# Attention, mixture of experts and MLP: differences of x staged over iterations, another order at the turn to the MLP

## The chip, the cores and the metric

The kernel runs on one core of a Trainium2 chip. The metric is the device time of one execution in microseconds (us). Engines are named TensorE (PE in the rows; PEld is its weight load), VectorE (DVE), ScalarE (ACT), GpSimd (POOL) and the SyncE queue that issues DMAs (SP).

## The reference

Attention with a window of 32 keys (half of the heads plain, half with a step of 4), then a mixture of four experts with all experts applied to all tokens, then an MLP with a sigmoid gate. Sizes: 2 x 576 tokens (1152), model width 512, expert width 1024, MLP width 2048.

```python
x = attention(q, k, v)                      # 1152 x 512
p = domain_probs / (domain_probs.sum(-1, keepdims=True) + 1e-9)
out = sum(p[:, e:e+1] * (np.maximum(x @ w1[e], 0) @ w2[e]) for e in range(4))
h = out @ w_in
y = (h * (1 / (1 + np.exp(-1.702 * h)))) @ w_out
```

## The kernel before

Every matmul operand is split into a high part (rounded to the type that TensorE multiplies) and a low part (the rest), and each product is three matmuls: high by high, high by low, low by high. ScalarE makes the high parts by a copy, VectorE or GpSimd the low parts by a subtraction. The program order of every engine is written out by hand; each engine runs its own queue in order, and semaphores tie them.

**First expert.** It runs in 26 iterations (`it`) along with the last steps of attention. Iteration `it` issues the products g1 of one pair (chunk of 384 tokens, 128 columns of the width), their relu on ScalarE (L498) with the low part on VectorE (L499), and the second matmul g2 (L514 to L516) of the pair issued two iterations before (`LAG = 2`). After that come the functions that `at_it(it, ...)` has listed, and `slot(1)`, which takes all that stands in the list `queue`.

**Experts 1 to 3 and the MLP.** A block (s, c) is a piece s of 256 columns of the width (s = 4 to 15 for the experts, 16 to 23 for the MLP; S0 is 15, SM is 16) with a token chunk c (512 or 640 tokens, as halves of 256 or 320). The first matmul of a block is made with seven products instead of eight, on sums and differences of the weights (`w1_prep`: sets A and S) and on x and its differences (`t`, made by `combos` and kept as `th`, `tl`). In a block `first2` issues the products a, c_, b, d, a, c_, d (names ga, gc, gb, gd in the rows, L735) into four banks of the five-bank pool `ps`; between them ScalarE copies s1 and s5, VectorE adds u2 (L751) and s75 (L753), and the second d goes into the bank that s75 has read. `second2` is the second matmul (L809 to L811) by tiles of 128 tokens, into three banks `pa0` to `pa2`; for the experts and most of the MLP VectorE adds a tile to `acc` (L813, L818), for s = 16 ScalarE copies it (L815). In the MLP the relu is replaced by a chain of tanh (L771), cc (L774), high copy (L775) and low part (L778).

**Work beside.** `due` gives each block or second matmul some lists of functions and a number of slots; `bg` mixes the lists evenly, and one slot follows each of the seven products of a `first2` and each tile of a `second2`. The 64-bit rounds (`w64_round`) turn the MLP's weights, which come as 64-bit numbers, into 32 bits: load, two ScalarE casts (L681, L682), a shift (L687) and a merge (L691) on VectorE, an add on GpSimd (L692), and a store of the round before. There are 32 units and 33 rounds.

**x1_combos** joins high and low of the attention result (GpSimd, L581), takes four differences (VectorE, L565), two high casts (ScalarE, L567) and two low parts (VectorE, L556), for chunk c and half m of the model width. **x2_turn** does the same for the MLP's x: transposes of `acc` (TensorE, L599), evictions (ScalarE, L603), high casts (L562), low parts and differences.

Buffers that matter: pool `big` has two tiles (a set of x1 takes both; `cc` of a block takes one), `sd` three, `m` two, `hp2` three.

Of the kernel before, what the change touches and what calls it, by code (L numbers as in the profile page):

```python
# [8 lines left out]
F32 = mybir.dt.float32  # L9
# [14 lines left out]
def fused_kernel(ctx: ExitStack, tc: tile.TileContext, q, k, v, dp, w1, w2, w_in, w_out, out):  # L24
# [37 lines left out]
    ps = ctx.enter_context(tc.tile_pool(name="ps", bufs=5, space=bass.MemoryType.PSUM))  # L62
    pacc = ctx.enter_context(tc.tile_pool(name="pacc", bufs=1, space=bass.MemoryType.PSUM))
# [13 lines left out]
    xh = xp.tile([P, KT, NT], F32R, name="xh")  # L77
    xl = xp.tile([P, KT, NT], F32R, name="xl")
# [3 lines left out]
    late = {}  # L82
# [351 lines left out]


    work = {}

    def at_it(it, fn):
        work.setdefault(it, []).append(fn)

    def close_attention():
        at.close()
        for nm, n in (("th", 1), ("ns", 5), ("ss", 1), ("cv", 2), ("sd", 3), ("big", 2)):
            late[nm] = ctx.enter_context(tc.tile_pool(name=nm, bufs=n))
        late["t"] = late["th"].tile([P, 2, 4, 2, NT // 2], F32R, name="t")

    p0, p1, p2, p3 = ORDER
# [18 lines left out]
    pa = {}  # L466
# [61 lines left out]
    NF = F1 // 2  # L528
    N_ = (256, 320)
# [5 lines left out]
    queue = []  # L535
# [12 lines left out]
    def combos(c, m, xf, t, whole, lo_engines=(nc.vector, nc.vector)):  # L548

        n, t0, q0 = N_[c], T0[c], Q0[c]  # L550
        th, tl = (late["t"][:, y, :, m, q0:q0 + n] for y in range(2))
        b = [xf[:, y] for y in range(4)]
        fns = []

        def lo_(eng, out_, whole_, hi_):
            eng.tensor_tensor(out=out_, in0=whole_, in1=hi_.bitcast(F32), op=ALU.subtract)  # L556

        if whole:
            for y, l in ((0, 0), (2, 0), (3, 1)):
                kt = 2 * (y // 2) + m  # L560
                cols = slice(t0 + l * n, t0 + (l + 1) * n)
                fns.append(lambda y=y, kt=kt, cols=cols: nc.scalar.activation(xh[:, kt, cols], b[y], AF.Copy))  # L562
                fns.append(lambda y=y, kt=kt, cols=cols: lo_(lo_engines[0], xl[:, kt, cols], b[y], xh[:, kt, cols]))
        for y, (p, q_) in enumerate(((b[1], b[0]), (b[3], t[:, 0]), (b[3], b[1]), (b[2], t[:, 1]))):
            fns.append(lambda y=y, p=p, q_=q_: nc.vector.tensor_tensor(out=t[:, y], in0=p, in1=q_, op=ALU.subtract))  # L565
        for ys in (slice(0, 2), slice(2, 4)):
            fns.append(lambda ys=ys: nc.scalar.activation(th[:, ys, :], t[:, ys], AF.Copy))  # L567
            fns.append(lambda ys=ys: lo_(lo_engines[1], tl[:, ys, :], t[:, ys], th[:, ys, :]))
        return fns

    def big_pair(c, name):
        return [late["big"].tile([P, 4, 320], F32, tag="big", name=f"{x}{name}")[:, :, :N_[c]] for x in ("xf", "xt")]

    def x1_combos(c, m):

        n, t0 = N_[c], T0[c]
        xf, t = big_pair(c, f"1_{c}{m}")

        def join(j):
            parts_ = [x.bitcast(F32)[:, 2 * j + m, t0:t0 + 2 * n].rearrange("p (l n) -> p l n", l=2) for x in (xh, xl)]  # L580
            nc.gpsimd.tensor_tensor(out=xf[:, 2 * j:2 * j + 2], in0=parts_[0], in1=parts_[1], op=ALU.add)  # L581
        return [lambda: join(0), lambda: join(1)] + combos(c, m, xf, t, False)

    def x2_turn(c, m):

        n = N_[c]
        if (c, m) == (0, 0):
            xf, t = big_pair(c, f"2_{c}{m}")
        else:
            both = late["hp"].tile([P, 8, n], F32, tag="h", name=f"x2_{c}{m}")  # L590
            xf, t = both[:, :4], both[:, 4:]

        def turn_tiles(j, x0, some):
            kt = 2 * j + m
            pool, tag = (ps, "ps") if c == 0 else (pacc, f"pa{turn_[0] % 3}")
            turn_[0] += c
            pt = pool.tile([P, 512], F32, tag=tag, name=f"x2_{c}{kt}{x0}")
            for i, tt in enumerate(some):
                nc.tensor.transpose(pt[:, i * P:(i + 1) * P], acc[:, tt, kt * P:(kt + 1) * P], ident)  # L599
            for h in range(2):  # L600
                lo_, hi_ = max(x0 * P, h * n), min((x0 + len(some)) * P, (h + 1) * n)
                if lo_ < hi_:
                    nc.scalar.activation(xf[:, 2 * j + h, lo_ - h * n:hi_ - h * n], pt[:, lo_ - x0 * P:hi_ - x0 * P], AF.Copy)  # L603

        tiles = TILES[c]
        pieces = ((0, tiles),) if c == 0 else ((0, tiles[:3]), (3, tiles[3:]))
        fns = [lambda j=j, x0=x0, some=some: turn_tiles(j, x0, some) for j in range(2) for x0, some in pieces]
        return fns + combos(c, m, xf, t, True, (nc.gpsimd, nc.vector if m == 0 or c else nc.gpsimd))


    def w1_prep(s):
# [21 lines left out]
    def w2_prep(s):  # L633
        t = wst[s, 1]
        hi, lo = (wa.tile([P, 2, DM], F32R, tag="w2", bufs=4, name=f"w2{y}_{s}") for y in "hl")
        wt[s, 1] = (hi, lo)
        fns = []
        for o in range(2):
            fns.append(lambda o=o: nc.scalar.activation(hi[:, o], t[:, o], AF.Copy))  # L639
            fns.append(lambda o=o: nc.gpsimd.tensor_tensor(out=lo[:, o], in0=t[:, o], in1=hi[:, o].bitcast(F32), op=ALU.subtract))  # L640
        return fns

    def prep1(s):
        return w1_prep(s) if s < SE else []
# [200 lines left out]
    for x, step in enumerate(steps[:FIRST]):  # L845
        step()
        spin(SPIN.get(x - LEAD, 0))
        for fn in first_work.get(x - LEAD, []):
            fn()
    for x in range(4):  # L850
        at_it(17 + x, lambda x=x: queue.extend(x1_combos(x % 2, x // 2)))
    at_it(15, lambda: queue.extend(loads(NF) + [units64[0][0], units64[1][0]] + loads(NF + 1)))
    at_it(20, lambda: queue.extend(w1_prep(NF)))
    at_it(22, lambda: queue.extend(w2_prep(NF)))
    for x in range(16, len(seq)):
        at_it(x, lambda: queue.extend(w64_round()))

    for it in range(len(seq) + LAG):
        it_now[0] = it
# [9 lines left out]
        slot(1)  # L869
    assert not work, sorted(work)  # L870
    first_expert.close()
    late["hp"] = ctx.enter_context(tc.tile_pool(name="hp2", bufs=3, side=RIGHT))

    def order_of(keys):
        pe = [("1", keys[0])]
        for x in range(1, len(keys)):
            pe += [("1", keys[x]), ("2", keys[x - 1])]
        return pe + [("2", keys[-1])]
# [4 lines left out]

    pe = pe[:pe.index(("1", (S0, 0))) + 1]
    pe += [("1", (S0, 1)), ("2", (S0, 0)), ("2", (S0 - 1, 1)), ("2", (S0, 1))]
    pe += order_of([(SM, 0), (SM + 1, 0), (SM, 1), (SM + 1, 1)] + [(s, c) for s in range(SM + 2, SE) for c in range(2)])

    def due(kind, s, c):

        one = 7 + (len(TILES[1 - c]) if (s, c) != (NF, 0) else 0)  # L890
        if kind == "1":
            r64 = w64_round()
            if (s, c) == (S0, 0):
                return 7, [prep1(SM), r64, loads(SM + 1)]
            if (s, c) == (S0, 1):
                return 7, [r64]
            if (s, c) == (SM, 0):
                return 7, [x2_turn(1, 0), prep2(SM + 1), r64]
            if (s, c) == (SM + 1, 0):
                return 7, [x2_turn(1, 1), loads(SM + 2)]  # L900
            if (s, c) == (SM, 1):
                return 7, [loads(SM + 3)]
            if (s, c) == (SM + 1, 1):
                return None
            if (s, c) == (SM + 2, 0):
                return one, [prep2(s) + prep1(s + 1), loads(s + 2)]
            return one, [prep1(s + 1), r64, loads(s + 2)] if c == 0 else [prep2(s + 1), r64]
        if (s, c) == (S0, 0):
            return 4, [prep1(SM + 1)]
        if (s, c) == (S0 - 1, 1):  # L910
            return 5, [x2_turn(0, 0)]
        if (s, c) == (S0, 1):
            return 5, [x2_turn(0, 1), prep2(SM)]
        if (s, c) == (SM + 1, 0):
            return 4 + 7 + 5, [prep1(SM + 2)]
        return None

    for kind, (s, c) in pe:
# [3 lines left out]
            left[0] = todo[0]  # L922
            bg(*todo[1])
        (first2 if kind == "1" else second2)(s, c, slots)
    assert not queue


_INS = ["q", "k", "v", "moe_domain_probs", "moe_w1", "moe_w2", "moe2_w_in", "moe2_w_out"]
# [25 lines left out]
```

## Time and profile before

| | |
|---|---|
| runs | 686.49 us median of 3 (684.76 to 686.67) |
| profiled execution | 687.18 us, span of its instructions 685.2 us |
| granted TensorE clock, mean | 0.980 |
| busy share of the span | TensorE 95%, VectorE 64%, GpSimd 53%, ScalarE 43% |

A busy share is a mean over stages. TensorE is the engine with the most work, so time is lost where it waits or where its granted clock is below 1.00 (1.00 is 2.4 GHz, the lower level is 1.2 GHz).

### The profile page before, as it was taken

To read this page: it belongs to the slowest core of one execution; us is meant where nothing else is said; L and a number is where in the kernel's file an instruction comes from. 1 tells how busy PE (TensorE), PEld (TensorE's weight loads), DVE (VectorE), ACT (ScalarE), POOL (GpSimd) and SP (SyncE) were. 2 spreads that over 40 slices of the span, in tenths; PEclk is the share of its full clock that TensorE was granted. 3 is DMA by queue.
4 is the path that set the end of the run, shared out by engine and by line. 5 is a ranking of instruction groups with operands and counts; after the bars stand their busy time and mean duration, and the time that the engine had idled before them with its cause. 6 is when DMAs were issued, how large, how long until landed. Compare 5 with 4: busy or idle time off the path is not lost. (4 is left out here: it accounts for less than half of the span.)

```text
span 685.2 us, 10981 instructions
## 1 busy us (share of the span) xinstructions
PE 651.6 (95%) x4059; PEld 572.3 (84%) x4059; DVE 438.1 (64%) x878; ACT 291.5 (43%) x674; POOL 365.9 (53%) x360
## 2 busy tenths in 40 slices
PE   8899999994899999999999999998689999999997
PEld 5688888882798989989898988887678989889895
DVE  4765443467677676676767567666755576666655
ACT  5765332235453443434344343445445543444321
POOL 4432210247797676676767567785523845744300
PEclk9999999997899999999999999999799999999999
DMA  8866000531662434253233415120000110100003
GB/s 212 208 172 164 27 1 1 200 90 49 187 200 78 136 107 131 70 154 109 79 121 112 145 51 183 49 94 31 32 0 32 62 63 32 62 1 1 1 0 139
DMA packets 50070, 61.41 MB, mean 90 GB/s; under 512 B 20514, under 2 KB 32482, under 8 KB 50018
## 3 DMA queue, kind: packets, MB, share of 16 engines
q1 hardware_dynamic: 50016, 60.72, 29.4%
q8 instruction: 32, 0.52, 0.3%
q14 instruction: 22, 0.16, 0.1%
HBM read 49.96 MB, written 10.75 MB: 89 GB/s over the span
## 5 line engine op out<-in xcount | busy, mean ns | idle before, releaser
L809 PE MATMUL q<-w2h,h 128*128 128x512 f32 x360 | 142.8, 397 | 2.1 <-ACT acc L815 2.1
L810 PE MATMUL q<-w2l,h 128*128 128x512 f32 x360 | 142.7, 396 | 0.0
L811 PE MATMUL q<-w2h,h 128*128 128x512 f32 x360 | 142.6, 396 | 0.0
L813 DVE SCALAR_TENSOR_TENSOR acc<-q,pw,acc 128x512 f32<-128x512 f32 x108 | 78.7, 745 | 29.2 <-PE q L811 29.1
L754 POOL TENSOR_TENSOR cc<-s,u 128x256 f32<-128x256 f32 (+1 forms) x40 | 35.8, 894 | 94.6 <-DVE s L753 94.6
L809 PEld LDWEIGHTS q<-w2h,h 128*128 128x128 f32 x360 | 67.8, 188 | 17.2 <-ACT acc L815 2.5
L811 PEld LDWEIGHTS q<-w2h,h 128*128 128x128 f32 x360 | 67.8, 188 | 16.5
L810 PEld LDWEIGHTS q<-w2l,h 128*128 128x128 f32 x360 | 67.8, 188 | 14.7
L640 POOL TENSOR_TENSOR w2l<-st,w2h 128x512 fp32r<-128x512 f32 x40 | 53.3, 1335 | 39.1 <-ACT w2h L639 39.1
L692 POOL TENSOR_TENSOR m<-m,sd 128x512 int32<-128x512 int32 x32 | 42.1, 1314 | 53.5 <-DMA st<-in_moe_w_dram 19.8
L629 POOL TENSOR_TENSOR wsl<-ss,wsh 128x512 fp32r<-128x512 f32 x40 | 61.6, 1559 | 13.7 <-ACT wsh L628 13.7
L747 ACT ACTIVATE s<-ga 128x256 f32<-128x256 f32 (+1 forms) x40 | 16.5, 412 | 119.2 <-PE ga L735 119.2
L751 DVE TENSOR_TENSOR u<-gb,s 128x256 f32<-128x256 f32 (+1 forms) x40 | 18.3, 458 | 65.0 <-PE gb L735 61.2
L818 DVE SCALAR_TENSOR_TENSOR acc<-q,acc 128x512 f32<-128x512 f32 x63 | 42.5, 687 | 13.9 <-PE q L811 13.9
L625 POOL TENSOR_TENSOR wal<-st,wah 128x512 fp32r<-128x512 f32 (+1 forms) x40 | 47.6, 1211 | 6.6 <-ACT wah L624 6.6
L735 PE MATMUL ga<-xh,wah 128*128 128x256 f32 (+1 forms) x160 | 47.9, 299 | 0.1
L735 PE MATMUL ga<-xl,wah 128*128 128x256 f32 (+1 forms) x160 | 47.7, 298 | 0.0
L735 PE MATMUL ga<-xh,wal 128*128 128x256 f32 (+1 forms) x160 | 47.5, 297 | 0.0
L767 DVE SCALAR_TENSOR_TENSOR h<-cc,h 128x768 fp32r<-128x768 f32 (+1 forms) x24 | 37.4, 1558 | 7.2 <-ACT h L764 7.2
L764 ACT ACTIVATE h<-cc 128x768 fp32r<-128x768 f32 (+1 forms) x24 | 22.3, 928 | 43.9 <-DVE cc L788 35.9
L514 PE MATMUL pa<-wh,h 128*128 128x512 f32 x72 | 31.8, 441 | 9.5 <-ACT h L498 9.5
L621 POOL TENSOR_TENSOR ss<-st 128x256 f32<-128x256 f32 x40 | 40.4, 1009 | 0.0
(457 smaller groups left out, 1653.4 us busy)
## 6 DMA issues: line engine op xcount, KB each, us to landing
st<-in_moe_w_dram SPq DMA_DIRECT2D x32, 512.0 KB, 5.5
sd<-in_moe_w_in_dram SPq DMA_DIRECT2D x16, 512.0 KB, 4.3
sd<-in_moe_w_out_dram SPq DMA_DIRECT2D x16, 512.0 KB, 4.0
w<-m SPq DMA_DIRECT2D x32, 256.0 KB, 4.6
st<-w SPq DMA_DIRECT2D x16, 512.0 KB, 3.2
out_dram<-acc SPq DMA_DIRECT2D x9, 256.0 KB, 2.0
v10big<-in_v_dram SPq DMA_DIRECT2D x2, 144.0 KB, 3.0
v11big<-in_v_dram SPq DMA_DIRECT2D x2, 144.0 KB, 2.4
```

Source lines behind the costliest of these rows:

```text
L621: fns.append(lambda y=y, p=p, q_=q_, op=op: nc.gpsimd.tensor_tensor(out=sums[:, y], in0=p, in1=q_, op=op))
L625: fns.append(lambda dst=dst, srcs=srcs: nc.gpsimd.tensor_tensor(out=al[:, dst], in0=srcs, in1=ah[:, dst].bitcast(F32), op=ALU.subtract))
L629: fns.append(lambda dst=dst: nc.gpsimd.tensor_tensor(out=sl[:, dst], in0=sums[:, dst], in1=sh[:, dst].bitcast(F32), op=ALU.subtract))
L640: fns.append(lambda o=o: nc.gpsimd.tensor_tensor(out=lo[:, o], in0=t[:, o], in1=hi[:, o].bitcast(F32), op=ALU.subtract))
L692: nc.gpsimd.tensor_tensor(out=m.bitcast(I32), in0=m.bitcast(I32), in1=t.bitcast(I32)[:, :, 0], op=ALU.add)
L735: nc.tensor.matmul(bank_[:, :n], wz[:, y, m, :], xz, start=start and m == 0 and z == 0, stop=m == 1 and z == 2, skip_group_check=not start)
L767: nc.vector.scalar_tensor_tensor(hl[:, sub], src, 0.0, hh[:, sub].bitcast(F32), op0=ALU.max, op1=ALU.subtract)
L809: nc.tensor.matmul(pt, hi, wh[:, o, :], start=o == 0, stop=False)
L810: nc.tensor.matmul(pt, hi, wl[:, o, :], start=False, stop=False)
L811: nc.tensor.matmul(pt, lo, wh[:, o, :], start=False, stop=o == 1)
L813: nc.vector.scalar_tensor_tensor(acc[:, t, :], pt, pw[:, t, e:e + 1], acc[:, t, :], op0=ALU.mult, op1=ALU.add)
L818: nc.vector.scalar_tensor_tensor(acc[:, t, :], pt, 0.5, acc[:, t, :], op0=ALU.mult, op1=ALU.add)
```

## The change

Four things. The differences of x for the experts (`x1_combos`) are spread over three iterations per set: join in one, differences in the next, casts and low parts in the one after, starting in iterations 16, 17, 19 and 20; the sets of m = 1 get a pool of their own, `x1`, which is closed with the first expert, and the pools `cv` and `sd` open only then. The weights of block (4,0) are prepared in iterations 21 to 24 by name, not through the list. The 64-bit rounds of iterations 16 to 23 and of the blocks from (15,1) on are gone; blocks with c = 1, from (4,1) to (14,1), take two rounds, those with c = 0, from (5,0) to (15,0), one. At the turn to the MLP the second matmul of (17,0) moves ahead of the block (16,1); the transposes of chunk 1, m = 0, come after three empty slots in (16,0), their casts and differences in (17,0); those of m = 1 come in the second matmuls of (16,0) and (17,0), with banks of `ps` instead of `pa0` to `pa2`. The weights of (18,0) are prepared in the 12 slots of (17,1) and the second matmul of (16,1), before in the 16 slots that began at the second matmul of (17,0).

```diff
-        for nm, n in (("th", 1), ("ns", 5), ("ss", 1), ("cv", 2), ("sd", 3), ("big", 2)):
+        for nm, n in (("th", 1), ("ns", 5), ("ss", 1), ("big", 2)):
             late[nm] = ctx.enter_context(tc.tile_pool(name=nm, bufs=n))
+        late["x1"] = x1_pool.enter_context(tc.tile_pool(name="x1", bufs=2))
...
+        def join():
+            xf, t = big_pair(c, f"1_{c}{m}", ("big", "x1")[m])
+            for j in range(2):
+                parts_ = [x.bitcast(F32)[:, 2 * j + m, t0:t0 + 2 * n].rearrange("p (l n) -> p l n", l=2) for x in (xh, xl)]
+                nc.gpsimd.tensor_tensor(out=xf[:, 2 * j:2 * j + 2], in0=parts_[0], in1=parts_[1], op=ALU.add)
+            made.extend(combos(c, m, xf, t, False))
...
+        at_it(it, join)
+        at_it(it + 1, lambda: some(0, 4))
+        at_it(it + 2, lambda: some(4, 8))
...
-            pool, tag = (ps, "ps") if c == 0 else (pacc, f"pa{turn_[0] % 3}")
-            turn_[0] += c
+            pool, tag = (pacc, f"pa{turn_[0] % 3}") if (c, m) == (1, 0) else (ps, "ps")
+            turn_[0] += (c, m) == (1, 0)
...
-    for x in range(4):
-        at_it(17 + x, lambda x=x: queue.extend(x1_combos(x % 2, x // 2)))
-    at_it(15, lambda: queue.extend(loads(NF) + [units64[0][0], units64[1][0]] + loads(NF + 1)))
-    at_it(20, lambda: queue.extend(w1_prep(NF)))
-    at_it(22, lambda: queue.extend(w2_prep(NF)))
-    for x in range(16, len(seq)):
-        at_it(x, lambda: queue.extend(w64_round()))
+    at_it(15, lambda: queue.extend(loads(NF) + loads(NF + 1)))
+    for x, (c, m, it) in enumerate(((0, 0, 16), (0, 1, 17), (1, 0, 19), (1, 1, 20))):
+        x1_combos(c, m, it)
...
+        for x, which in enumerate(((0, 1, 2, 3, 4, 6), (5, 7, 8, 10), (9, 11))):
+            at_it(it + x, lambda which=which: some(*which))
+        at_it(it + 3, lambda: [fn() for fn in w2_prep(NF)])
+
+    first_weights(21)
...
-    pe += order_of([(SM, 0), (SM + 1, 0), (SM, 1), (SM + 1, 1)] + [(s, c) for s in range(SM + 2, SE) for c in range(2)])
+
+    pe += [("1", (SM, 0)), ("1", (SM + 1, 0)), ("2", (SM, 0)), ("2", (SM + 1, 0)), ("1", (SM, 1))]
+    pe += order_of([(SM, 1), (SM + 1, 1)] + [(s, c) for s in range(SM + 2, SE) for c in range(2)])[1:]
...
-            r64 = w64_round()
+            if (s, c) == (NF, 0):
+                return one, [prep1(s + 1), loads(s + 2) + [units64[0][0], units64[1][0]]]
+            r64 = [fn for _ in range(1 + c) for fn in w64_round()] if (s, c) <= (S0, 0) else []
...
             if (s, c) == (SM, 0):
-                return 7, [x2_turn(1, 0), prep2(SM + 1), r64]
+                turns.extend(x2_turn(1, 0))
+                return 7, [[nothing] * 3 + turns[0], prep2(SM + 1)]
             if (s, c) == (SM + 1, 0):
-                return 7, [x2_turn(1, 1), loads(SM + 2)]
+                return 7, [turns[1], loads(SM + 2)]
...
             if (s, c) == (SM + 1, 1):
-                return None
+                return one + 1, [prep1(SM + 2)]
...
+        if (s, c) == (SM, 0):
+            turns[:] = x2_turn(1, 1)
+            return 4, [turns[0]]
         if (s, c) == (SM + 1, 0):
-            return 4 + 7 + 5, [prep1(SM + 2)]
+            return 4, [turns[1]]
```

## Rows read from the trace of the kernel before

**Rows 1.** Page, busy tenths in 40 slices of 17.1 us, TensorE.
```profile
PE   8899999994899999999999999998689999999997
```
**Rows 2.** Waits of TensorE, whole span: total us, times, longest.
```profile
PE pa L514 <- ACT h L498: 9.5, 2, 6.4
PE x L599 <- ACT x L603: 6.3, 1, 6.3
PE pa L516 <- DVE h L499: 3.0, 3, 1.7
PE gd L735 <- DVE s L753: 2.2, 3, 1.1
PE q L809 <- ACT acc L815: 2.1, 1, 2.1
PE x L599 <- DVE acc L813: 1.9, 1, 1.9
```
**Rows 3.** Windows: length, busy us of each engine, granted clock, DMA.
```profile
148.55:181.67 33.12, 20.60 (x70) 15.19 (x70) 20.16 (x26) 12.83 (x24) 23.95 (x19) 0.79 0.32 95
473.00:512.20 39.20, 28.93 (x171) 27.05 (x170) 23.59 (x38) 19.83 (x46) 16.52 (x16) 0.83 0.08 27
307.53:319.30 11.77, 11.77 (x68) 10.67 (x67) 7.82 (x12) 4.47 (x8) 7.29 (x7) 1.00 0.22 77
```
**Rows 4.** Timeline of TensorE, first turn: start us, us, then idle before.
```profile
144.36 0.39 PE L514 MATMUL pa<-wh,h 128*128 128x512 f32 x1
...
148.55 0.39 PE L514 MATMUL pa<-wh,h 128*128 128x512 f32 x1
...
156.50 0.80 PE L514 MATMUL pa<-wh,h 128*128 128x512 f32 x1 [3.08 <-ACT h L498]
...
181.67 0.28 PE L735 MATMUL ga<-xh,wah 128*128 128x256 f32 x1
```
**Rows 5.** Timelines of GpSimd, VectorE and ScalarE, first turn.
```profile
150.29 2.54 POOL L581 TENSOR_TENSOR xf<-xh,xl 128x512 f32<-128x512 f32 x2
...
151.61 1.50 DVE L565 TENSOR_TENSOR xt<-xf 128x256 f32<-128x256 f32 x1 [2.24 <-POOL xf L581]
...
153.67 1.30 ACT L567 ACTIVATE t<-xt 128x512 fp32r<-128x512 f32 x2 [5.58 <-DVE xt L565]
...
155.97 0.47 ACT L498 ACTIVATE h<-g 128x384 fp32r<-128x384 f32 x1
```
**Rows 6.** Timelines of VectorE and TensorE, one odd block.
```profile
311.31 0.49 DVE L753 TENSOR_TENSOR s<-gd,s 128x320 f32<-128x320 f32 x1 [0.39 <-PE gd L735]
311.72 0.42 DVE L687 TENSOR_SCALAR m<-sd 128x512 uint32<-128x512 uint32 x1
...
313.41 0.68 DVE L691 SCALAR_TENSOR_TENSOR m<-sd,m 128x512 uint32<-128x512 uint32 x1
...
312.81 0.46 PE L735 MATMUL gd<-t,wah 128*128 128x320 f32 x2
```
**Rows 7.** Timeline of VectorE, blocks (15,0) and (15,1).
```profile
441.20 1.75 DVE L691 SCALAR_TENSOR_TENSOR m<-sd,m 128x512 uint32<-128x512 uint32 x1
...
447.55 1.47 DVE L687 TENSOR_SCALAR m<-sd 128x512 uint32<-128x512 uint32 x1
```
**Rows 8.** Chain that ended last, in order of time: start us, us.
```profile
458.76 0.87 PE x L599 x8
...
543.21 0.88 PE ga L735 x6
...
554.97 0.72 PE ga L735 x6
```
**Rows 9.** Timelines of GpSimd, ScalarE and VectorE, second turn.
```profile
476.57 1.28 POOL L556 TENSOR_TENSOR t<-x,t 128x512 fp32r<-128x512 f32 x1
...
488.26 0.84 ACT L771 ACTIVATE th<-cc 128x768 f32<-128x768 f32 x1 [2.56 <-DVE cc L788]
...
491.01 0.96 DVE L778 TENSOR_TENSOR h<-cc,h 128x768 fp32r<-128x768 f32 x1 [0.91 <-ACT h L775]
```

More of the change, by code (lines that the diff above doesn't have):

```diff
@@ L436, in fused_kernel @@
     work = {}
+    x1_pool = ExitStack()
     def at_it(it, fn):
@@ L569, in combos, with big_pair, x1_combos, some @@
         return fns
-    def big_pair(c, name):
-        return [late["big"].tile([P, 4, 320], F32, tag="big", name=f"{x}{name}")[:, :, :N_[c]] for x in ("xf", "xt")]
-    def x1_combos(c, m):
+    def big_pair(c, name, pool="big"):
+        return [late[pool].tile([P, 4, 320], F32, tag=pool, name=f"{x}{name}")[:, :, :N_[c]] for x in ("xf", "xt")]
+    def x1_combos(c, m, it):
         n, t0 = N_[c], T0[c]
[L577 to L582, printed above, removed]
+        made = []
+        def join():
[4 more added lines that the diff above has]
+            made.extend(combos(c, m, xf, t, False))
+        def some(a_, b_):
+            for fn in made[a_:b_]:
+                fn()
+        at_it(it, join)
+        at_it(it + 1, lambda: some(0, 4))
+        at_it(it + 2, lambda: some(4, 8))
     def x2_turn(c, m):
@@ L607, in x2_turn @@
         fns = [lambda j=j, x0=x0, some=some: turn_tiles(j, x0, some) for j in range(2) for x0, some in pieces]
-        return fns + combos(c, m, xf, t, True, (nc.gpsimd, nc.vector if m == 0 or c else nc.gpsimd))
+        return fns, combos(c, m, xf, t, True, (nc.gpsimd, nc.vector if m == 0 or c else nc.gpsimd))
     def w1_prep(s):
@@ L849, in fused_kernel, with first_weights, some @@
             fn()
-    for x in range(4):
-        at_it(17 + x, lambda x=x: queue.extend(x1_combos(x % 2, x // 2)))
-    at_it(15, lambda: queue.extend(loads(NF) + [units64[0][0], units64[1][0]] + loads(NF + 1)))
-    at_it(20, lambda: queue.extend(w1_prep(NF)))
-    at_it(22, lambda: queue.extend(w2_prep(NF)))
-    for x in range(16, len(seq)):
-        at_it(x, lambda: queue.extend(w64_round()))
+    at_it(15, lambda: queue.extend(loads(NF) + loads(NF + 1)))
+    for x, (c, m, it) in enumerate(((0, 0, 16), (0, 1, 17), (1, 0, 19), (1, 1, 20))):
+        x1_combos(c, m, it)
+    def first_weights(it):
+        made = []
+        def some(*which):
+            made.extend([] if made else w1_prep(NF))
+            for x in which:
+                made[x]()
+        for x, which in enumerate(((0, 1, 2, 3, 4, 6), (5, 7, 8, 10), (9, 11))):
+            at_it(it + x, lambda which=which: some(*which))
+        at_it(it + 3, lambda: [fn() for fn in w2_prep(NF)])
+    first_weights(21)
     for it in range(len(seq) + LAG):
@@ L871, in fused_kernel @@
     first_expert.close()
+    x1_pool.close()
+    for nm, n in (("cv", 2), ("sd", 3)):
+        late[nm] = ctx.enter_context(tc.tile_pool(name=nm, bufs=n))
     late["hp"] = ctx.enter_context(tc.tile_pool(name="hp2", bufs=3, side=RIGHT))
@@ L885, in fused_kernel, with nothing @@
     pe += [("1", (S0, 1)), ("2", (S0, 0)), ("2", (S0 - 1, 1)), ("2", (S0, 1))]
-    pe += order_of([(SM, 0), (SM + 1, 0), (SM, 1), (SM + 1, 1)] + [(s, c) for s in range(SM + 2, SE) for c in range(2)])
+    pe += [("1", (SM, 0)), ("1", (SM + 1, 0)), ("2", (SM, 0)), ("2", (SM + 1, 0)), ("1", (SM, 1))]
+    pe += order_of([(SM, 1), (SM + 1, 1)] + [(s, c) for s in range(SM + 2, SE) for c in range(2)])[1:]
+    turns = []
+    def nothing():
+        pass
     def due(kind, s, c):
@@ L895, in due @@
             if (s, c) == (S0, 1):
-                return 7, [r64]
+                return None
             if (s, c) == (SM, 0):
-                return 7, [x2_turn(1, 0), prep2(SM + 1), r64]
+                turns.extend(x2_turn(1, 0))
+                return 7, [[nothing] * 3 + turns[0], prep2(SM + 1)]
             if (s, c) == (SM + 1, 0):
-                return 7, [x2_turn(1, 1), loads(SM + 2)]
+                return 7, [turns[1], loads(SM + 2)]
             if (s, c) == (SM, 1):
@@ L910, in due @@
         if (s, c) == (S0 - 1, 1):
-            return 5, [x2_turn(0, 0)]
+            return 5, [sum(x2_turn(0, 0), [])]
         if (s, c) == (S0, 1):
-            return 5, [x2_turn(0, 1), prep2(SM)]
+            return 5, [sum(x2_turn(0, 1), []), prep2(SM)]
+        if (s, c) == (SM, 0):
+            turns[:] = x2_turn(1, 1)
+            return 4, [turns[0]]
         if (s, c) == (SM + 1, 0):
-            return 4 + 7 + 5, [prep1(SM + 2)]
+            return 4, [turns[1]]
         return None
@@ L924, in fused_kernel @@
         (first2 if kind == "1" else second2)(s, c, slots)
-    assert not queue
+    assert not queue and at64[0] == len(units64) + 1
 _INS = ["q", "k", "v", "moe_domain_probs", "moe_w1", "moe_w2", "moe2_w_in", "moe2_w_out"]
```

## The prediction

> **What bounds the kernel now.** I read the page first, then the waits of TensorE, then timelines around each place where it waits. The 40 slices [rows 1] show TensorE busy nearly everywhere and two holes: the tenth slice, where the first expert ends, and slices 28 to 30, the turn to the MLP. The list of what TensorE waited for [rows 2] puts causes to them: 9.5 us on ScalarE's relu of the first expert (L498) with 3.0 us on VectorE's low part (L499), then 6.3, 2.1 and 1.9 us on instructions of the second turn, and 2.2 us on VectorE's s75 (L753) in three pieces, which lie in the product blocks of (4,0), (15,0) and (15,1). Between the holes nothing waits: the stretch of an odd block, 307.53 to 319.30, has TensorE busy for all of its 11.77 us, at a granted clock of 1.00, with VectorE at 7.8 and GpSimd at 7.3 [rows 3]. So a gain can only come out of the holes, and a loss only out of new waits in the full stretch.
>
> **First turn, what is removed.** One iteration takes 148.55 - 144.36 = 4.19 us of TensorE, half for the next products, half for the second matmul of the iteration two before. From 148.55 the rest is five second matmuls and two products: 7 halves of 2.1 us, 14.7 us, so the experts' blocks could begin at 163.2. They begin at 181.67 [rows 4]. 18.4 us are lost: 12.5 us of waits [rows 2] and the rest at the lower clock, granted 0.79 over the stretch, a part of it at 1.2 GHz, against 1.00 in the full one [rows 3]. The reason is the order of ScalarE's queue. `slot(1)` empties the whole list each iteration, so join (GpSimd), four differences (VectorE), two high casts (ScalarE) and the 64-bit round stand ahead of the next relu. In [rows 5] the join starts at 150.29, the first difference at 151.61, the high casts wait 5.58 us for differences and start at 153.67, and the relu runs at 155.97; the second matmul behind it starts at 156.50 [rows 4]. The fourth burst does the same, with the weights of block (4,0) on top.
>
> **First turn, what takes its place.** Now the join of a set is issued in one iteration, its differences in the next, its casts in the one after. A relu is needed two iterations (8.4 us) after its products end, so what stands ahead of it may take some 8 us more than the 4.19 us that come free each time. The fullest iterations are 18 to 22. In 18 and 19 VectorE has two low parts, four differences and one relu low part. Priced from [rows 5], where the first difference beside a join took 1.50 us, four differences are 6 us at the very worst; two low parts and the relu's, each some 0.7 us (the merge of [rows 6] is of their size), make it 8 us once, and the next iteration has no differences. ScalarE never waits more than one such pile. The third join waits for the casts of the first set to release their buffers, which ends one iteration earlier; the fourth likewise, in the extra pool. The weights of block (4,0) come in iterations 21 to 24; GpSimd's part (its 23.95 us of the stretch [rows 3] less four halves of joins at 1.27 and five adds at 1.3 to 1.5: some 12 us) starts once the fourth join is through, near 147, and ends near 163, with the low part of S needed at 163.9 and w2 not before 174. The loads of iteration 15 keep their place and have fewer DMAs around them. I take the whole 18.4 us. Bounds: 18.4, and 9 if half of the burst stays because a release comes late.
>
> **The 64-bit rounds.** Eight rounds leave the first expert, two the blocks (15,0), (15,1) and one the first block (4,0). Their 22 instructions of VectorE and the adds of GpSimd go to odd blocks (4,1) to (14,1), two rounds each. Where they are taken away, the three s75 waits go: 2.2 us [rows 2]. Where they are added, the question is TensorE's second `gd`, which needs s75. Now s75 starts at 311.31, takes 0.49, and `gd` starts at 312.81: a slack of 1.0 us [rows 6]. With the 14 functions over 11 slots the first round's shift (0.42) and merge (0.68) come between the second and third product, ahead of u2 and s75. The shift waits for ScalarE's two casts, so the pair ends near 311.3, u2 near 311.75, s75 near 312.2: slack 0.6 us, no wait. The second round falls between the drains of the second matmul, where VectorE has 11.77 - 7.82 = 4 us to spare [rows 3] for 1.1 us more. GpSimd goes from 7.3 to 8.6 us of the odd block's 11.77 (one add more, 1.3 by the instruction of its size in [rows 9]) and the even blocks keep their work; behind the second add stand w2's low part and the next sums, which have a block pair to their use. The SP queue waits for a stage buffer until the first round's add is done; behind it stand a store and weight loads needed a block pair later. I take 0 and keep both ends: nothing, and what the stretched pair costs, below.
>
> The row that speaks against this: beside a GpSimd instruction the same shift took 1.47 us and the merge 1.75 us [rows 7], together 2.1 us more than in [rows 6]; less the slack of 0.6 this is 1.5 us of waiting in each of 11 odd blocks, 16 us. It needs GpSimd still at work on the S low parts at that moment; by my times it stops 1 to 2 us earlier. The Trainium skill, "SBUF — State Buffer", section "Who interferes with whom", says that a VectorE instruction with two SBUF inputs and a GpSimd instruction that reads SBUF shut each other out, the later one standing until the earlier has ended. By that rule either step would be held for up to one whole GpSimd instruction, and the sum would be rival C's; the rows of the stretched pair agree with it in kind.
>
> **Second turn.** In 473.0 to 512.2 TensorE has work for 14 products of 0.72, 7 of 0.88 [rows 8], four tiles (11.77 less 7 of 0.88, over 4: 1.40 each) and twenty transposes, 2.2 us (eight took 0.87 [rows 8]): 24.1 us of 39.2. 10.3 us are waits [rows 2], the other 4.8 us lower clock (granted 0.83 [rows 3]): three drops of some 1.5 us. The largest wait, 6.3 us, is a transpose whose bank is released by an eviction that stands on ScalarE behind tanh, and that behind VectorE's differences: tanh at 488.26, last gate step at 491.01 [rows 9].
>
> The new order spreads the transposes of (1,0) behind three empty slots, gives its differences the block (17,0), and puts (1,1)'s transposes and differences under the second matmuls of 16 and 17, with spare banks of the five-bank pool. That takes away the 1.9, the 6.3 and the 2.1. Following the queues by the durations of before, five waits come in their place:
> 1. The second product of (16,0) needs the (0,1) low parts, formerly hidden by the 1.9 us: until 475.2, 1.5 us.
> 2. Its fourth product needs the second half, which GpSimd ends at 477.85 [rows 9]: 0.9 us.
> 3. In block (17,0) ScalarE is still in the gate chain of (16,0) (3.7 us from tanh to the last step [rows 9]), then does two casts before s1, which `ga` needs: 2.5 us.
> 4. VectorE then has three differences beside GpSimd's low parts ahead of s75: 2.0 us.
> 5. Block (16,1) needs the low part of (1,1)'s first two differences. VectorE comes to it after four drains and four differences, near 509.4, while TensorE is there at 506.4: 3.1 us.
>
> 10.0 us of waits and two clock drops (behind 3 with 4, and 5) of 1.5 us: 13.0 us against 15.1 us: a gain of 2.1 us. The bounds are wide: none of the five and no drop, +15.1; all with five drops, 17.5 us, -2.4. I take 2.1, since each of the five follows from a queue that I could write down.
>
> **Sum.** 18.4 + 2.2 + 0 + 2.1 = 22.7 us. The profiled execution took 687.18 us (span 685.2 and 2.0 around it): 664.5. The median of the runs, 686.49, lies 0.7 below the profiled one: **663.8 us**.
>
> **The rivals.**
> A, forecast: chance 0.63; its own range is 658 to 668, by the second turn's gain between -2.4 and +8.
> B: the second turn gives nearly all. For it: the empty slots and the spare banks take evictions off TensorE's path; against it: waits 3 to 5 rest on chains that are only moved. 8 to 13 us more: 651 to 656. 0.10.
> C: the double rounds hold TensorE in the odd blocks, by 0.3 to 1.5 us each, 11 times: 667 to 680. For it, [rows 7] and a slack of 0.6; against it, GpSimd's pause at that time. 0.14.
> D, the other side: as C, but each wait is long enough to drop the clock, as the three of the second turn did. 1.5 of waiting and 1.5 of lower clock, 11 times: 33 us, 697. It outweighs the gain from 22.7 / 11 = 2.1 us per odd block. Against it: the three waits on s75, 0.7 us each in the mean [rows 2], are far shorter than the 1.9 us of the shortest wait in the second turn. 0.05.
> E: the change doesn't do what it says: the staged sets still pile up in front of the relu, by buffers or by GpSimd's order. Half of the 18.4 stays: 673 (0.06); all of it and nothing elsewhere: no change (0.02).
>
> Range: A with C's lower half and B's upper edge, 656 to 674; outside lie most of B, C's upper third, half of E, and D, near 0.2. About 0.3%, 2 us, is what a measurement of this kernel can tell from none. Faster: A, B, C and the half of E, 0.93; same 0.02; slower 0.05.
>
> **What would show it.** Right: no wait on L498 or L499 behind 148 us, and block (4,0) at 163 us, clock 1.00 there; no wait on s75 in blocks 4 to 15; in the second turn waits of 1 to 3 us on ScalarE's and VectorE's copies instead of one of 6 us, and block (17,1) some 2 us nearer to block (16,0). Wrong: s75 waits in the odd blocks 24 us apart (C, D); relus late in iterations 19 to 23 (E); a second turn with TensorE busy throughout (B), or with more waits than 13 us.

## The result and the profile after

The changed kernel took 659.77 us (median of 4 runs, 659.19 to 660.52) against 685.90 for the one before: ratio 0.962, 95% interval 0.960 to 0.964, or 26.1 us less. Forecast were 663.8 us, 22.7 less, in a range of 656 to 674. The profiled spans are 657.4 and 685.2 us.

The page of the changed kernel: TensorE and its granted clock in 40 slices of 16.4 us. The hole of [rows 1] in the tenth slice is closed; the second is shallower.

```profile
PE   9899999999999999999999999999789999999997
...
PEclk9999999999999999999999999999999999999999
```

The waits of TensorE in the changed kernel (total us, times, longest), as in [rows 2]. The relu (L500 now), the evictions and the copies are gone. s1 (L759), s75 (L765) and the low parts of the turn (L558) have come up. Of the three waits on s75 one, of 1.9 us, lies in the second turn; the other two, of 0.6 and 0.2 us, lie in blocks (4,1) and (15,1).

```profile
PE ga L747 <- ACT s L759: 3.4, 2, 2.0
PE gd L747 <- DVE s L765: 2.7, 3, 1.9
...
PE gc L747 <- DVE t L558: 1.0, 1, 1.0
PE gc L747 <- POOL t L558: 0.9, 1, 0.9
...
PE gd L747 <- POOL t L558: 0.7, 1, 0.7
```

Windows of the changed kernel for the three stretches of [rows 3] (same columns): the first turn from the same second matmul to block (4,0), the second from block (16,0) to block (17,1), and an odd block.

```profile
147.11:161.72 14.61, 14.61 (x70) 12.66 (x70) 10.60 (x15) 7.12 (x13) 10.34 (x9) 1.00 0.11 37
450.71:488.03 37.32, 30.87 (x196) 27.44 (x194) 24.76 (x42) 19.84 (x46) 15.83 (x16) 1.00 0.09 29
310.58:322.35 11.77, 11.77 (x68) 10.68 (x67) 8.08 (x14) 5.56 (x10) 4.59 (x5) 1.00 0.43 129
```

The first turn takes 14.61 us (forecast 14.7, 33.12 before) with TensorE busy for all of it. The odd block takes 11.77 us as before, with both rounds in it. The spans part as follows, by the starts of the blocks in the two timelines and the end of attention's last product:

| stretch | before | after | difference | forecast |
|---|---|---|---|---|
| start to the end of attention | 122.41 | 120.96 | -1.45 | 0 |
| to block (4,0) | 59.26 | 40.76 | -18.50 | -18.4 |
| to block (16,0) | 291.32 | 288.99 | -2.33 | -2.2 |
| to block (17,1) | 44.83 | 37.32 | -7.51 | -2.1 |
| to the end | 167.38 | 169.37 | +1.99 | 0 |

The first line isn't touched by the change; it varies by execution (121.0 to 122.5 us in most profiles here, 126.3 and 127.5 in two). Without it the spans differ by 26.3 us, close to the medians' 26.1. So in these two profiles the forecast was short at the second turn, by 3.4 us net (5.5 against 2.1).

### The profile page after: what moved, and what is told of

It is laid out like the page before. It is cut to its first block, busy times and chain, and to the rows that moved or that the text cites. A ratio compares the mean times of both kernels' runs of the same rounds, so it can differ in the third digit from the quotient of the medians.

```text
span 657.4 us, 11002 instructions
## 1 busy us (share of the span) xinstructions
PE 641.6 (98%) x4059; PEld 565.4 (86%) x4059; DVE 419.4 (64%) x878; ACT 291.1 (44%) x674; POOL 352.7 (54%) x360
## 4 chain that ended last, share of the span: by engine, by line
PE 88%; DVE 5%; ACT 3%; POOL 1%; issue 1%; DMA 1%; DVEq 0%; ACTq 0%; POOLq 0%
PE q L821 12%; PE q L822 12%; PE q L823 12%; PE gd L747 9%; PE ga L747 9%; PE gc L747 8%; PE g L488 7%; PE gb L747 4%; PE pa L516 3%; PE pa L518 3%; PE pa L517 3%; DVE x L567 1%; DVE cc L786 1%; PE spin L389 1%; DMA rawq03small<-in_q_dram 1%
## 5 line engine op out<-in xcount | busy, mean ns | idle before, releaser
L825 DVE SCALAR_TENSOR_TENSOR acc<-q,pw,acc 128x512 f32<-128x512 f32 x108 | 80.8, 748 | 38.5 <-PE q L823 37.0
L823 PEld LDWEIGHTS q<-w2h,h 128*128 128x128 f32 x360 | 67.8, 188 | 16.4
L641 POOL TENSOR_TENSOR wsl<-ss,wsh 128x512 fp32r<-128x512 f32 x40 | 53.3, 1353 | 20.5 <-ACT wsh L640 20.5
L637 POOL TENSOR_TENSOR wal<-st,wah 128x512 fp32r<-128x512 f32 (+1 forms) x40 | 49.5, 1256 | 1.7 <-ACT wah L636 1.7
L759 ACT ACTIVATE s<-ga 128x256 f32<-128x256 f32 (+1 forms) x40 | 16.3, 408 | 74.2 <-PE ga L747 74.2
L651 ACT ACTIVATE w2h<-st 128x512 fp32r<-128x512 f32 x40 | 25.1, 631 | 48.7 <-PE q L822 48.7
L747 PE MATMUL gd<-t,wah 128*128 128x256 f32 (+1 forms) x160 | 33.5, 298 | 2.7 <-DVE s L765 2.7
L790 DVE TENSOR_TENSOR h<-cc,h 128x256 fp32r<-128x256 f32 (+3 forms) x32 | 28.9, 903 | 10.7 <-ACT h L787 9.1
L747 PE MATMUL gc<-t,wsh 128*128 128x256 f32 (+1 forms) x160 | 33.7, 297 | 2.0 <-DVE t L558 1.0
```

The lines of the kernel that those rows point to most:

```text
L637: fns.append(lambda dst=dst, srcs=srcs: nc.gpsimd.tensor_tensor(out=al[:, dst], in0=srcs, in1=ah[:, dst].bitcast(F32), op=ALU.subtract))
L641: fns.append(lambda dst=dst: nc.gpsimd.tensor_tensor(out=sl[:, dst], in0=sums[:, dst], in1=sh[:, dst].bitcast(F32), op=ALU.subtract))
L747: nc.tensor.matmul(bank_[:, :n], wz[:, y, m, :], xz, start=start and m == 0 and z == 0, stop=m == 1 and z == 2, skip_group_check=not start)
L823: nc.tensor.matmul(pt, lo, wh[:, o, :], start=False, stop=o == 1)
L825: nc.vector.scalar_tensor_tensor(acc[:, t, :], pt, pw[:, t, e:e + 1], acc[:, t, :], op0=ALU.mult, op1=ALU.add)
```

## The experiments

**The two turns apart.** First, the changed kernel with the order, banks and slots of before at the turn to the MLP:

```diff
-    pe += [("1", (SM, 0)), ("1", (SM + 1, 0)), ("2", (SM, 0)), ("2", (SM + 1, 0)), ("1", (SM, 1))]
-    pe += order_of([(SM, 1), (SM + 1, 1)] + ...)[1:]
+    pe += order_of([(SM, 0), (SM + 1, 0), (SM, 1), (SM + 1, 1)] + ...)
...
-            pool, tag = (pacc, f"pa{turn_[0] % 3}") if (c, m) == (1, 0) else (ps, "ps")
+            pool, tag = (ps, "ps") if c == 0 else (pacc, f"pa{turn_[0] % 3}")
...
```

> The changed first expert and the moved rounds with the old order, banks and slots at the turn to the MLP. Theory from the two profiles (the second turn gained 8.1 us between the start of block (16,0) and that of (17,1), and 2.0 us came back later): 6 us above the changed kernel, near 666, with the waits of 6.3, 2.1 and 1.9 us of before. Rival, the size that the prediction gave the second turn: 2 us above, near 662.

663.7 us, ratio 0.9688 (0.9669 to 0.9707): between theory and rival; 21.4 us of the gain are the first turn and the rounds. Waits and window of its second turn, and under it the window of the same stretch in the kernel before:

```profile
PE x L611 <- ACT x L615: 7.0, 1, 7.0
PE x L611 <- DVE acc L825: 1.9, 1, 1.9
PE q L821 <- ACT acc L827: 1.4, 1, 1.4
```
```profile
451.50:494.25 42.75, 32.40 (x195) 29.37 (x194) 28.45 (x43) 22.01 (x49) 19.40 (x19) 0.92 0.08 25
```
```profile
472.99:517.82 44.83, 34.56 (x195) 31.59 (x194) 28.30 (x43) 22.37 (x49) 19.10 (x19) 0.85 0.07 24
```

The waits of before are back, but the stretch takes 42.75 us, not 44.83, at a granted clock of 0.92 instead of 0.85. In stretches of 2 us the clock of the kernel before falls in three places, around or behind each of its three long waits; here it falls in one, around the wait of 7.0 us.

Second, the converse: `x1_combos`, the weights of (4,0) and the rounds as before, the new turn to the MLP. The lines are set against the changed kernel.

```diff
-    at_it(15, lambda: queue.extend(loads(NF) + loads(NF + 1)))
-    for x, (c, m, it) in enumerate(((0, 0, 16), (0, 1, 17), (1, 0, 19), (1, 1, 20))):
-        x1_combos(c, m, it)
+    for x in range(4):
+        at_it(17 + x, lambda x=x: queue.extend(x1_combos(x % 2, x // 2)))
...
+    for x in range(16, len(seq)):
+        at_it(x, lambda: queue.extend(w64_round()))
```

> The first expert and the rounds of before with the new order, banks and slots at the turn to the MLP. Theory: 6 us below the kernel before, near 680, the waits of the second turn as in the changed kernel (7 to 8 us) and no clock drop there. Rival, the prediction's size: 2 us below, near 684, with two drops of the clock.

682.85 us, ratio 0.9962 (0.9949 to 0.9975), 2.6 us less: near the forecast's 2.1, far from the 5.5 of the table and from the theory's 6. One reason stands in its window of the second turn: the waits start where those of the changed kernel do, but the clock fell once, which makes 1.4 us. Another is that the table's profile of the kernel before is a long execution, 687.18 us, 2.3 above the median of its runs beside this one.

```profile
472.46:511.15 38.69, 33.22 (x195) 29.31 (x194) 24.05 (x42) 20.07 (x46) 15.84 (x16) 0.91 0.08 28
```

**Staging or rounds.** Third, the rounds moved, each set in one iteration again, with the weights of (4,0) through the list:

```diff
+    for x in range(4):
+        at_it(17 + x, lambda x=x: queue.extend(x1_combos(x % 2, x // 2)))
+    at_it(20, lambda: queue.extend(w1_prep(NF)))
+    at_it(22, lambda: queue.extend(w2_prep(NF)))
...
-        at_it(it, join)
-        at_it(it + 1, lambda: some(0, 4))
-        at_it(it + 2, lambda: some(4, 8))
```

> The changed kernel with the sets of differences issued each in one iteration again, from the one pair of buffers, and the weights of (4,0) through the list, but without the 64-bit rounds in the first expert. Theory, the staging is needed: a burst still takes 6 to 7 us against 4.19 us of an iteration, so relus come late from the third set on and 4 to 8 us of the 18.4 stay: 664 to 668. Rival, the rounds alone made the burst too long: within 1.5 us of the changed kernel, 660 to 661.

662.96 us, ratio 0.9672 (0.9653 to 0.9690), between theory and rival: 1.4 us of the first turn stay, not 4 to 8. Of the relu's waits one of 1.0 us is left; timeline of TensorE in this run, attention's last product and the first of block (4,0):

```profile
122.52 0.92 PE L319 MATMUL pv11big<-pT11big,v11big 96*64 96x64 f32 x24
...
158.24 0.51 PE L515 MATMUL pa<-wh,h 128*128 128x512 f32 x1 [0.99 <-ACT h L499]
...
164.68 0.28 PE L737 MATMUL ga<-xh,wah 128*128 128x256 f32 x1
```

Fourth, staging with the rounds left where they were. Space allows one pair of buffers for the sets then, so they start in iterations 16, 18, 20 and 22. Fifth, to tell the pair from the rounds, the changed kernel with the one pair:

```diff
-    for x, (c, m, it) in enumerate(((0, 0, 16), (0, 1, 17), (1, 0, 19), (1, 1, 20))):
+    for x, (c, m, it) in enumerate(((0, 0, 16), (0, 1, 18), (1, 0, 20), (1, 1, 22))):
...
-            xf, t = big_pair(c, f"1_{c}{m}", ("big", "x1")[m])
+            xf, t = big_pair(c, f"1_{c}{m}", "big")
```

> The converse: the sets staged over three iterations (one pair of buffers, so they start in iterations 16, 18, 20 and 22) with the eight 64-bit rounds left in the first expert and one round per block after it; the new turn to the MLP. Theory, staging does most: 2.2 us of waits on s75 come back and up to 3 us of late relus: 662 to 666. Rival, the rounds do most: 670 or more.

> The changed kernel with the staged sets made in the one pair of buffers, starting in iterations 16, 18, 20 and 22, so that each join is issued beside the low parts of the set before. It differs from the run with the rounds kept only by the rounds and the weights' list. Theory, the rounds cost the time there: within 2 us of the changed kernel, 660 to 662. Rival, the one pair costs it (joins beside low parts, last set late): 666 or more.

676.87 us, ratio 0.9881 (0.9860 to 0.9903), where the rival is right and staging does not do most, and 664.27 us, ratio 0.9702 (0.9670 to 0.9735), between theory and rival. The weights of (4,0) are prepared by name in both, so the rounds, with the place of their pools, are the difference between them. Timelines of TensorE, first with the rounds kept, then with the one pair alone:

```profile
121.91 0.92 PE L319 MATMUL pv11big<-pT11big,v11big 96*64 96x64 f32 x24
...
168.05 0.80 PE L517 MATMUL pa<-wh,h 128*128 128x512 f32 x1 [5.25 <-DVE h L500]
...
171.21 0.41 PE L746 MATMUL ga<-xh,wah 128*128 128x256 f32 x1
...
179.62 0.53 PE L746 MATMUL gd<-t,wah 128*128 128x256 f32 x2 [2.85 <-DVE s L764]
```
```profile
127.45 0.92 PE L319 MATMUL pv11big<-pT11big,v11big 96*64 96x64 f32 x24
...
168.21 0.28 PE L746 MATMUL ga<-xh,wah 128*128 128x256 f32 x1
```

From the end of attention to block (4,0) the four cases take, in us:

| | rounds in the first expert | rounds moved |
|---|---|---|
| each set in one iteration | 59.26 (before) | 42.16 (third run) |
| sets staged | 49.30 (fourth) | 40.76 (changed; 40.76 with one pair) |

Staged stands here for both: the sets over three iterations and the weights by name, which no run parts. Moving the rounds alone gives 17.1 of the 18.5 us, staging alone 10.0; with the rounds gone staging is worth 1.4 here. The fourth run shows why. TensorE waits there for VectorE's low part of h, not for the relu; timeline of VectorE:

```profile
147.51 3.69 DVE L557 TENSOR_TENSOR t<-xt,t 128x512 fp32r<-128x512 f32 x2
151.12 1.79 DVE L698 TENSOR_SCALAR m<-sd 128x512 uint32<-128x512 uint32 x1
152.94 0.69 DVE L702 SCALAR_TENSOR_TENSOR m<-sd,m 128x512 uint32<-128x512 uint32 x1
```

Two low parts beside an add and a join of GpSimd take 3.69 us and the shift 1.79 (0.42 in [rows 6]), so VectorE needs more than the 4.19 us of an iteration. The one pair costs nothing up to block (4,0); behind it that run has 3.1 us of waits in block (4,1), against 0.6 in the changed kernel, and from (4,0) to (16,0) it takes 291.90 us against 288.99, 2.9 us of its distance.

**Where the doubled rounds lie.**

```diff
-            r64 = [fn for _ in range(1 + c) for fn in w64_round()] if (s, c) <= (S0, 0) else []
+            r64 = [fn for _ in range(2 - c) for fn in w64_round()] if (s, c) <= (S0, 0) else []
```

> The changed kernel with two 64-bit rounds in the blocks with c = 0 and one in those with c = 1, the other way round. Theory of the prediction (a pair of shift and merge beside GpSimd's low parts is stretched and makes s75 late): c = 0 blocks have GpSimd busy for 9.1 of 12.06 us, so s75 comes 0.4 to 1.1 us after the second gd could start, in 11 blocks: 4 to 12 us above the changed kernel, 664 to 672. Rival: the place of the rounds does not matter once they have left the first expert: 660.

660.66 us, ratio 0.966 (0.962 to 0.970): no difference that can be told from the changed kernel. The times alone don't exclude 4 or 5 us, since one of the four runs took 665.05 us; the trace does: from block (4,0) to (16,0) this run takes 288.37 us, the changed kernel 288.99. Its waits in that stretch:

```profile
PE gd L747 <- DVE s L765: 0.4, 1, 0.4
```

In an even block (298.73 to 310.79) of the rounds only the first shift stands ahead of s75; GpSimd pauses beside it, and it takes 0.43 us. Both merges come later. So this run doesn't price a stretched pair ahead of s75; block (4,1) of the changed kernel, below, shows a stretched shift there. The condition of the expectation did not hold either: GpSimd is busy for 7.4 us of the even blocks here, not 9.1. The run shows that the even blocks have room too.

**The second turn.** The changed kernel with s1 issued ahead of the rest of the gate chain, and then also with the casts and differences of (17,0) later in that block:

```diff
-        while deferred:
-            deferred.pop(0)()
         product(a, A, 0, 0, 0, True)
         nc.scalar.activation(s1, a[:, :n], AF.Copy)
+        while deferred:
+            deferred.pop(0)()
...
-                return 7, [turns[1], loads(SM + 2)]
+                return 7, [[nothing] * 8 + turns[1], loads(SM + 2)]
```

> The changed kernel with the rest of the gate chain of the block before issued after s1 instead of ahead of the first product. Theory, ScalarE's order causes the waits on s1: the 1.43 us in (17,1) go, 1.4 to 1.7 us; the 1.96 us in (17,0) only move to s75, which VectorE sets there: 658. Rival, s1 waits for something else: no change.

> The run with s1 first, and eight empty slots ahead of the casts and differences in block (17,0), so that VectorE has no difference ahead of s75. Theory, the differences ahead of s75 cause that wait: the 1.88 and the 1.96 us go too, 3 to 5 us below the changed kernel in all, 655 to 657. Rival, the work only moves on: the wait of block (16,1) for the low part of (1,1), 1.03 us now, grows by as much: 658.

661.16 us, ratio 0.9654 (0.9630 to 0.9678), and 659.72 us, 0.9633 (0.9609 to 0.9657): no gain that the times show from either, and neither forecast (658; 655 to 657) came true. The waits on s1 are gone in both. In the first they are back as a 2.4 us wait on s75, and its stretch took 38.89 us at a granted clock of 0.91; in the second the wait on s75 is 0.4 us, and instead the second matmul waits for ScalarE's copies of tiles, which now stand behind the later evictions and casts. Waits in the second turn of the second step, and its window:

```profile
PE q L821 <- ACT acc L827: 1.8, 2, 1.4
PE gc L747 <- DVE t L558: 0.9, 1, 0.9
```
```profile
451.28:487.94 36.66, 31.42 (x196) 27.51 (x195) 24.32 (x42) 19.73 (x46) 15.86 (x16) 1.00 0.09 30
```

0.66 us less than the changed kernel's 37.32. The work only moved on, but not to where the rival had it: the wait of block (16,1) is 0.9 us instead of 1.0.

Then banks and empty slots, beside the changed kernel once more:

```diff
-            pool, tag = (pacc, f"pa{turn_[0] % 3}") if (c, m) == (1, 0) else (ps, "ps")
+            pool, tag = (ps, "ps") if c == 0 else (pacc, f"pa{turn_[0] % 3}")
```
```diff
-                return 7, [[nothing] * 3 + turns[0], prep2(SM + 1)]
+                return 7, [turns[0], prep2(SM + 1)]
```

> The changed kernel once more, beside the two runs below on the same chip. 0.962 of the kernel before. In six profiles of this second turn the clock stayed at 1.00 twice (37.3 us from (16,0) to (17,1)) and fell to 0.91 four times (38.3 to 39.1 us) with the same waits; theory, the drop is a matter of the single execution: its turn is one of the two; rival, it goes with the kernel: 37.3 us at 1.00 again.

> The changed kernel with the transposes of (1,1) on the three banks of the second matmul again. Theory, the banks matter: tiles and transposes of the second matmuls of (16,0) and (17,0) take turns on three banks, and ScalarE evicts each 2 to 3 us after it is ready, so TensorE waits 2 to 6 us there: 662 to 666. Rival, the other order alone gives it: under 1 us.

> The changed kernel without the three empty slots ahead of the transposes of (1,0). Theory, the transposes meet sums that VectorE has not yet added, and the 1.9 us wait of before comes back in place of the 0.92 and 0.65 us on GpSimd's low parts: 0.3 to 1.0 us above the changed kernel. Rival, no difference above 0.3 us.

The changed kernel: 660.76 us, 0.9653 (0.9631 to 0.9676). Old banks: 662.97 us, 0.9683 (0.9656 to 0.9709). No empty slots: 659.75 us, 0.9633 (0.9610 to 0.9656). The intervals overlap. The old banks' median lies at the lower end of the theory's 662 to 666, so the trace has to decide there. Windows of the second turn, one from each profile, in this order:

```profile
450.96:489.16 38.20, 32.46 (x196) 28.67 (x194) 24.06 (x42) 20.02 (x46) 15.83 (x16) 0.96 0.08 29
```
```profile
456.04:495.25 39.21, 33.39 (x195) 29.24 (x194) 24.03 (x42) 20.13 (x46) 15.82 (x16) 0.91 0.08 28
```
```profile
450.81:487.73 36.92, 31.11 (x195) 27.45 (x194) 24.76 (x42) 19.73 (x46) 15.88 (x16) 1.00 0.08 30
```

The clock fell in the first two, in the first for a shorter time than in any profile so far, so the outcome there was neither of the two kinds. The old banks make one wait of 0.2 us on an eviction, not 2 to 6; their longer stretch has the lower clock. Without the empty slots VectorE's sum is waited for by 0.3 us, not 1.9, the two waits on GpSimd's low parts shrink to 0.6 and 0.2, and the stretch is 0.4 us shorter than the 37.32 us of the changed kernel at the same clock. By their waits neither part matters much.

## Why the prediction was right, and where its sizes were off

**First turn: right in size, and partly for another reason.** 18.5 us against 18.4; block (4,0) followed 14.61 us of work with the clock at 1.00. The prediction named the pile ahead of the relu and counted the 64-bit round as one part of it, but it looked for the cure in the staging and treated the rounds as a matter of the blocks that receive them. The table of four cases shows the rounds as the larger share: without them a set made in one iteration is late once, by 1.0 us. Neither part's gain adds to the other's, since both shorten one pile.

**Two sizes inside it were misplaced.** The differences were priced at 1.50 us beside a join. In the changed kernel those of chunk 0 took 0.42 us and those of chunk 1 from 0.48 to 1.58, beside GpSimd's work on the weights; it is the low parts of chunk 0 that meet the next join (timeline of VectorE, changed kernel):

```profile
135.77 3.61 DVE L558 TENSOR_TENSOR t<-xt,t 128x512 fp32r<-128x512 f32 x2
139.31 0.41 DVE L567 TENSOR_TENSOR xt<-xf 128x256 f32<-128x256 f32 x1
...
141.30 3.88 DVE L558 TENSOR_TENSOR t<-xt,t 128x512 fp32r<-128x512 f32 x2
```

3.61 and 3.88 us for two, where 1.4 were reckoned. By the schedule the full iterations are 18 and 21, not 18 and 19: a set's low parts meet the next set's differences only there. Low parts, differences and the relu's low part of iteration 18 take 5.8 us, under the 8 us allowed, so the conclusion held.

**The s75 waits and the odd blocks: right in size, with one block as the rival had it.** 2.33 us came out between blocks (4,0) and (16,0) (forecast 2.2). The waits of (4,0) and (15,0) are gone, that of (15,1) fell from 0.7 to 0.2 us, and one of 0.6 us is new in (4,1); the sign "no wait on s75 in blocks 4 to 15" is not quite met. In the odd blocks from (5,1) to (14,1) there is none. In the one of the window above s75 ends 0.7 us ahead of the second `gd` (forecast 0.6); timelines of VectorE and TensorE:

```profile
313.69 0.69 DVE L703 SCALAR_TENSOR_TENSOR m<-sd,m 128x512 uint32<-128x512 uint32 x1
314.30 0.48 DVE L763 TENSOR_TENSOR u<-gb,s 128x320 f32<-128x320 f32 x1
314.70 0.48 DVE L765 TENSOR_TENSOR s<-gd,s 128x320 f32<-128x320 f32 x1
...
315.85 0.46 PE L747 MATMUL gd<-t,wah 128*128 128x320 f32 x2
```

GpSimd had stopped 1.8 us before the shift (forecast 1 to 2), and the merge ran in 0.69 us. Block (4,1) is the other case. There GpSimd works on a low part of w2 until 171.05, the shift beside it takes 1.02 us, and s75 comes late:

```profile
170.31 1.02 DVE L699 TENSOR_SCALAR m<-sd 128x512 uint32<-128x512 uint32 x1 [0.42 <-ACT sd L694]
...
172.26 0.48 DVE L765 TENSOR_TENSOR s<-gd,s 128x320 f32<-128x320 f32 x1
...
172.79 0.56 PE L747 MATMUL gd<-t,wah 128*128 128x320 f32 x2 [0.60 <-DVE s L765]
```

That is rival C's wait, once instead of 11 times. That it stayed at one is in part luck: GpSimd was forecast at 8.6 us of an odd block with the even ones as before, but it fell from 7.3 to 4.6 us in the odd blocks and rose from 9.1 to 12.0 of 12.06 us in the even ones, as the mix of the lists shifts with their length; in the run with the doubled rounds in the even blocks it went the other way, 9.7 and 7.4. The window of the even block ahead of the odd one above:

```profile
298.52:310.58 12.06, 12.06 (x73) 10.69 (x72) 7.96 (x14) 5.02 (x11) 11.98 (x12) 1.00 0.50 159
```

D found no place: the granted clock stays at 1.00 behind the wait in (4,1). E found none either: the relus are on time.

**Second turn: the five waits right in kind, their sizes and the clock drops not.** The step was "10.0 us of waits and two clock drops of 1.5 us". All five waits are there in the order of the list; timeline of TensorE with its waits, then VectorE ahead of s75:

```profile
452.97 0.39 PE L747 MATMUL gc<-t,wsh 128*128 128x256 f32 x1 [0.92 <-POOL t L558]
...
455.64 0.39 PE L747 MATMUL gd<-t,wsh 128*128 128x256 f32 x1 [0.65 <-POOL t L558]
...
463.88 0.39 PE L747 MATMUL ga<-xh,wah 128*128 128x256 f32 x1 [1.96 <-ACT s L759]
...
467.45 0.50 PE L747 MATMUL gd<-t,wah 128*128 128x256 f32 x2 [1.88 <-DVE s L765]
...
483.23 0.41 PE L747 MATMUL gc<-t,wsh 128*128 128x320 f32 x1 [1.03 <-DVE t L558]
...
493.14 0.42 PE L747 MATMUL ga<-xh,wah 128*128 128x320 f32 x1 [1.43 <-ACT s L759]
```
```profile
462.87 0.96 DVE L790 TENSOR_TENSOR h<-cc,h 128x768 fp32r<-128x768 f32 x1 [0.91 <-ACT h L787]
463.75 1.16 DVE L567 TENSOR_TENSOR x<-x 128x320 f32<-128x320 f32 x1
464.84 0.41 DVE L763 TENSOR_TENSOR u<-gb,s 128x256 f32<-128x256 f32 x1
465.17 1.89 DVE L567 TENSOR_TENSOR x<-x 128x320 f32<-128x320 f32 x2
466.99 0.41 DVE L765 TENSOR_TENSOR s<-gd,s 128x256 f32<-128x256 f32 x1
```

0.92, 0.65, 1.96, 1.88 and 1.03 us stand against 1.5, 0.9, 2.5, 2.0 and 3.1: 6.4 us, not 10.0. The last is a third of its forecast: (1,1)'s differences took 2.7 us in all, and the four drains (VectorE's adds of tiles to `acc`) 0.69 us each, ahead of it. A sixth wait, 1.43 us on s1 in (17,1), was not listed, though it has the cause of the third: a block that follows a block finds ScalarE in the gate chain of the one before; the run with s1 first, in which both are gone, shows it. It lies behind the start of (17,1) and makes most of the last row of the first table. And the clock didn't fall at all in this profile; where it fell in other profiles of this turn it fell once, never behind the wait of (16,1) as forecast. The sum: 37.32 us less 29.7 of work (the 24.1 and four tiles more at 1.40) leave 7.6, with the 2.0 behind (17,1) 9.6 us, against 13.0: 3.4 less, which is the distance of the first table. It is a net of misses both ways: 3.6 too much for the five waits and 3.0 for two drops, 1.4 too little for the sixth wait and 1.7 for what TensorE loses in starting again after the six. The 1.7 is a difference, 9.6 less 7.9 of waits. The timeline bears it out: around the 1.43 us wait three matmuls start at 491.40, 493.14 and 493.39, where without one they start 0.15 us apart, so 1.7 us are lost, 0.26 more than the wait. With the same 29.7 us the old turn lost 15.1, as forecast.

How much the second turn is worth therefore depends on the pair of executions: 2.6 us alone by the ratio of the second run; with the other parts in place, 0.9688 for the old turn against 0.962 and 0.965 for the new, 2.4 to 4.6 us. The forecast's 2.1 lies just below these; the 5.5 of the first table is above them.

## What to carry to other kernels

When an engine's queue is late at one place, list all that stands ahead in it and ask which part need not be there at all: work that is not needed soon (the 64-bit rounds) is moved first, and spreading the rest may then be worth little. Read the destination's slack where a later product needs an earlier sum, not its busy share; here 0.7 us of slack was enough wherever GpSimd paused, and not in the one odd block where it was still at work. When a list gets longer, look at what the mix does to the other engines' work as well. Waits that come from one chain through three engines move when the order changes; a change of order pays what it shortens in the chain, not what it removes in front of TensorE.

## What had not been expected of the hardware

The clock: the turn's code is the same in the changed kernel, its second profile, the second to fifth runs and the one with the doubled rounds in even blocks (the second and fourth have one more store, a DMA, in (16,0)), and its first three waits are alike to 0.02 us. After waits of up to 2.0 us the granted clock of that stretch was 1.00 twice (37.32 and 37.33 us), 0.96 once (38.20) and 0.91 four times (38.30, 38.64, 38.69 and 39.10). Each time it fell once, to 0.50 in stretches of 2 us (0.57 in the profile with 0.96, where it was short), behind the wait of 1.96 us in (17,0) or the one on s75 that follows. So waits of this length may drop the clock to its lower level, 1.2 GHz, or not, with the same code, and the stretch is 0.9 to 1.8 us longer when they do. A part is paid back: the wait of (16,1), 1.03 us at the full clock, is 0.3 to 0.7 us then. Of the nine executions of the changed kernel on record six have a mean clock of 1.00 over the whole span, the others 0.995 or 0.996. The Trainium skill, "TensorE: Matmul & The Clock Gate", section "What's actually happening", says that the gate's setting follows how busy TensorE has recently been, by a window that runs on its own; that agrees with the same waits ending either way, and no run here shows the window itself.

Low parts of VectorE (128x512, from two arrays in SBUF) and joins of GpSimd (640 columns) that run beside each other were longer on both engines. From 135.29 us in the changed kernel join, low part, join and low part start in this order, each while the one before runs, and take 1.57, 1.64, 2.01 and 2.05 us; alone a join takes 1.54 us and a low part 0.7. The Trainium skill, "SBUF — State Buffer", section "Who interferes with whom", has the later of two such instructions stand until the earlier has ended. This agrees: the first of the four is as long as alone, and each of the others ends 0.5 us (a low part) or 1.4 us (a join) after the one before it.
